# GateLoop attention and a SoLU feed-forward: second product by 32 tokens on groups of array columns, z turned without gaps, and the first chain taken per batch

## The chip, the cores and the metric

The kernel runs on one core of one Trainium2 chip, in one launch. The metric is the time of one execution on the device in microseconds (us). The engines have these names in the profile: PE is TensorE (PEld its weight loads), DVE is VectorE, ACT is ScalarE, POOL is GpSimd, SP is SyncE, which issues most of the DMA transfers. L1068 means line 1068 of the kernel before.

## What is computed

A gated linear attention with a complex decay for each of 8 heads of width 48, then a feed-forward block on its output, all in float32:

```python
B, H, S, D = 4, 8, 768, 48
mag = sqrt(a_re**2 + a_im**2)
scale = minimum(mag, 0.999) / (mag + 1e-6)
a_re_n, a_im_n = a_re * scale, a_im * scale
for t in range(S):                                   # state S_re, S_im: (B, H, D, D)
    new_re = ar * S_re - ai * S_im                   # ar, ai: step t of a_re_n, a_im_n
    new_im = ar * S_im + ai * S_re
    S_re, S_im = new_re + outer(k[t], v[t]), new_im
    y[t] = q[t] @ S_re

x = y.transpose(0, 2, 1, 3).reshape(3072, 384)
h = x @ w_in                                         # 384 -> 1024
sm = softmax(h, axis=-1)
solu = h * sm
ln = (solu - mean(solu)) / sqrt(var(solu) + 1e-6) * g_ln
out = ln @ w_out                                     # 1024 -> 384
```

## The kernel before

The work is cut into 24 chunks of 128 tokens (6 stretches of time for each of 4 batches). A group g of two chunks shares the preparation of the decays: a chain of elementwise steps between DVE and ACT that turns `a_re` and `a_im` into logarithms and angles, then running sums over the 128 tokens as products with a triangular matrix, then exponentials, cosine and sine.

```python
        def clamp():
            for nm in ("lr", "x0", "u"):
                st[nm] = tmp.tile([P, GW], FP, tag=nm, name=f"f_{nm}")      # GW = 768: two chunks of 384
            ar, ai = st["ar"], st["ai"] = flat(T["ar", g]), flat(T["ai", g])
            nc.vector.tensor_scalar(out=ar, in0=ar, scalar1=LEAST, scalar2=None, op0=OP.max, op1=OP.max,
                                    accum_out=seen[:, 1, g:g + 1])
            nc.vector.tensor_scalar(out=ai, in0=ai, scalar1=1e15, scalar2=-1e15, op0=OP.min, op1=OP.max)

        def inverse():
            nc.scalar.activation(out=st["lr"], in_=st["ar"], func=AF.Ln)
            nc.scalar.activation(out=st["x0"], in_=st["lr"], func=AF.Exp, scale=-1.0)

        def ratio():
            ar, ai, x0 = (st[nm] for nm in ("ar", "ai", "x0"))
            nc.vector.tensor_tensor(out=ai, in0=ai, in1=x0, op=OP.mult)
            nc.vector.tensor_tensor(out=x0, in0=ar, in1=x0, op=OP.mult)

        def tangent():
            ai, x0 = st["ai"], st["x0"]
            nc.vector.scalar_tensor_tensor(out=x0, in0=x0, scalar=2.0, in1=ai, op0=OP.subtract, op1=OP.mult)
            nc.vector.tensor_scalar(out=x0, in0=x0, scalar1=1.5, scalar2=-1.5, op0=OP.min, op1=OP.max)
        # [cut: square, secant, size, eps, lnm, fourth: further steps of the chain on the same 768 columns]

        def total(i):                                   # running sum of chunk i of the group
            ps = st["L", i] = ps_t.tile([P, DM], FP, tag="t", padded_shape=[P, 512], name="f_L")
            nc.tensor.matmul(out=ps, lhsT=tri, rhs=st["lr"][:, i * DM:(i + 1) * DM], start=True, stop=True)
```

For the products with k and q, both are transposed: DVE transposes blocks of 32x32 (`f_kb`), and four DMA transfers put the blocks in place (`f_kqT`). Only chunks 0 and 1 are transposed on PE. `score` and `values` then compute the attention on four groups of 32 array columns each: the outputs of four consecutive matmuls lie in four different groups of 32 partitions.

```python
        def values():
            # [cut: lists the matmuls of each of the four column groups in queues]
                    queues[p % 4].append(dict(out=y[r:r + w, c0:c0 + P], lhsT=lhsT, rhs=rhs, start=(k == 0),
                                              stop=(k == len(todo) - 1)))     # r = p % 4 * 32
            for todo in zip(*queues):
                for product in todo:
                    nc.tensor.matmul(**product)
```

The feed-forward block of a chunk n: the first product (`up`, weights x, streamed `w_in`), exp on ACT, z = h * exp on DVE (`solu`). z is transposed for the second product, in most chunks by DVE and DMA (`blocks`, `away`), in the chunks of `SHORT` on PE (`turn_z`). The second product (`down`) has the transposed z as weights and streams `w_out`. The mean of z over its 1024 columns is taken out beforehand by centring `w_out` (`mean`, `centre`), and the row scale is applied at the end (`scale`).

```python
    SHORT = [0, 1, 2, 23]

        def blocks():
            st["zb"] = zbp.tile([P, 4, 32, KF], FP, tag="zb", name="f_zb")        # KF = 8
            nc.vector.transpose(out=st["zb"].rearrange("p s t c -> p s c t"),
                                in_=st["z"].rearrange("p (c f s) -> p s c f", s=4, f=32))

        def away():
            st["zT"] = zp.tile([P, 4, 32, KF], FP, tag="zT", name="f_zT")
            for r in range(4):
                nc.sync.dma_start(out=st["zT"][:, r].rearrange("p t c -> p (t c)"),
                                  in_=st["zb"][r * 32:(r + 1) * 32].rearrange("p s t c -> p s (t c)"))

        def down(half):
            if half == 0:
                st["o"] = ps_o.tile([P, DM], FP, tag="o", padded_shape=[P, 512], name="f_o")
            for c in range(half * KF // 2, (half + 1) * KF // 2):
                nc.tensor.matmul(out=st["o"], lhsT=st["zT"][:, c] if n in SHORT else st["zT"].rearrange("p r t c -> p (r t) c")[:, :, c], rhs=w_out[:, c],
                                 start=(c == 0), stop=(c == KF - 1))
```

`mean` has eight matmuls with all 128 array columns, whose weights are one column of `g_ln` repeated:

```python
        def mean(c):
            if c == 0:
                gs = T["gs"] = const.tile([P, KF], FP, name="f_gs")
                nc.vector.tensor_scalar(out=gs, in0=g_ln, scalar1=1.0 / FF, scalar2=None, op0=OP.mult)
                T["mean"] = ps_o.tile([P, DM], FP, tag="o", padded_shape=[P, 512], name="f_mean")
            nc.tensor.matmul(out=T["mean"], lhsT=T["gs"][:, c:c + 1].to_broadcast([P, P]), rhs=w_out[:, c],
                             start=(c == 0), stop=(c == KF - 1))
```

The order in which these steps are put into the engines' queues is written down: `START`, then `EVEN` and `ODD` in turn for n = 2 to 19, then `END`. A name such as `down0:-1` stands for step `down0` of chunk n - 1, and `clamp:g2` for step `clamp` of the group two after that of n. Each engine takes its own instructions in that order. `again` and `inspect` read the weights a second time for a check of their range, and a verdict at the end selects a general version of the kernel where inputs are outside of the fast one's range.

Of the kernel before, what the change touches and what calls it, by code (L numbers as in the profile page):

```python
# [11 lines left out]
FP = mybir.dt.float32  # L12
# [503 lines left out]
load_ar:0 load_ai:0 fetch:9 fetch:13 fetch:5 clamp:0 fetch:11 inverse:0 ratio:0 raised:9 raised:13 tangent:0  # L516
fetch:2 convert:9 square:0 secant:0 size:0 fetch:0 load_k:0 raised:11 eps:0 convert:13 lnm:0 fetch:1 fourth:0
total0:0 load_ar:1 raised:0 total1:0 raised:5 decay0:0 grow1:0 grow0:0 decay1:0 convert:11 trig:0 angle:0
convert:5 convert:0 ks1:0 phase0:0 raised:2 phase1:0 last:0 ks0:0 load_q:0 nearest0:0 gain:0 nearest1:0 ends:0
load_ai:1 load_v:0 convert:2 raised:1 part0:0 part1:0 fetch:7 cos:0 convert:1 qs0:0 turn_ends:0 tot:0 clamp:1  # L520
sin:0 k2:0 exp:0 q2:0 kt0:0 inverse:1 kT0:0 qt0:0 fetch:3 k2:1 fetch:4 qs1:0 ratio:1 kt1:0 load_vr:0 qT0:0
raised:7 kT1:0 qt1:0 qT1:0 q2:1 carry:1 kt0:1 score1:0 raised:3 fetch:10 convert:7 fetch:6 kT0:1 fetch:12 add:1
fetch:8 raised:4 score0:0 load_k:1 mask0:0 load_ai:2 kt1:1 tangent:1 load_q:1 qt0:1 values:0 convert:3 qT0:1
kT1:1 qt1:1 turned_x:0 carry:0 square:1 qT1:1 secant:1 up0:0 raised:6 convert:4 up1:0 raised:8 size:1 load_ar:2
eps:1 score1:1 load_vr:2 fourth:1 raised:10 score0:1 convert:6 raised:12 convert:8 lnm:1 total0:1 convert:10
grow0:1 decay0:1 total1:1 load_v:1 grow1:1 mean:0 convert:12 ks0:1 mean:1 mean:2 mean:3 decay1:1 mean:4 exp0:0
mask0:1 mean:5 trig:1 qs0:1 angle:1 phase0:1 add:0 nearest0:1 phase1:1 solu0:0 nearest1:1 ks1:1 last:1 mean:6
centred:0 qs1:1 mean:7 values:1 clamp:2 part0:1 part1:1 zt1:0 cos:1 sin:1 centre:0 exp:1 centre:1 load_k:2
turned_x:1 zt0:0 centre:4 load_vr:1 centre:3 up0:1 inverse:2 up1:1 centre:2 centre:5 centre:7 zT0:0 k2:2
centre:6 q2:2 ratio:2 spread:0 tangent:2 load_ai:3 zT1:0 kqb:2 square:2 secant:2 kqt0:2 down0:0 size:2 k2:3 q2:3  # L530
down1:0 eps:2 exp0:1 load_q:2 lnm:2 fourth:2 total1:2 total0:2 kqb:3 solu0:1 grow1:2 decay1:2 kqt0:3 ends:1
score0:2 centred:1 grow0:2 score1:2 decay0:2 turn_ends:1 tot:1 last:2 zt0:1 mask0:2 zt1:1 load_ar:3 values:2
qs1:2 score0:3 score1:3 trig:2 angle:2 zT0:1 turned_x:2 on:2 ks1:2 zT1:1 mask0:3 phase0:2 norm:0 load_v:2
spread:1 phase1:2 ks0:2 scale:0 qs0:2 nearest0:2
"""
EVEN = """
nearest1:g1 mask0:1 carry:0 part0:g1 ks1:g1 load_q:g2 part1:g1 cos:g1 clamp:g2 up0:0 sin:g1 up1:0 load_k:g2
add:0 exp:g1 values:1 inverse:g2 k2:2 exp0:0 down0:-1 q2:2 kqb:2 turned_x:1 ratio:g2 solu0:0 tangent:g2
load_v:g2 square:g2 load_ar:g3 blocks:0 carry:1 secant:g2 size:g2 k2:3
"""  # L540
ODD = """
kqt0:1 down1:-2 q2:2 eps:g2 load_ai:g3 up0:0 up1:0 add:0 fourth:g2 centred:-1 zt0:-1 zt1:-1 zT0:-1 away:-1
norm:-2 scale:-2 again:-4 score0:1 zT1:-1 lnm:g2 store:-3 score1:1 exp0:0 spread:-1 kqb:2 solu0:0 total1:g2
decay1:g2 total0:g2 decay0:g2 mask0:1 down0:-1 blocks:0 again:-3 ends:g1 grow0:g2 qs0:g2 load_vr:g2 down1:-1
last:g2 kqt0:2 grow1:g2 centred:0 turn_ends:g1 values:1 trig:g2 inspect:-3 ks0:g2 angle:g2 score0:2 store:-2
on:g2 spread:0 inspect:-6 tot:g1 score1:2 away:0 norm:-1 phase0:g2 qs1:g2 turned_x:1 scale:-1 phase1:g2
nearest0:g2
"""
END = """
mask0:21 down0:19 nearest1:11 store:18 part0:11 part1:11 cos:11 sin:11 norm:19 k2:22 up0:20 q2:22 up1:20 exp:11  # L550
kqb:22 ks1:11 values:21 exp0:20 down1:19 solu0:20 turned_x:21 kqt0:22 score0:22 k2:23 q2:23 kqb:23 up0:21
scale:19 blocks:20 kqt0:23 score1:22 up1:21 mask0:22 exp0:21 score0:23 centred:20 away:20 solu0:21 score1:23
values:22 mask0:23 blocks:21 centred:21 spread:20 down0:20 turned_x:22 norm:20 up0:22 store:19 down1:20
spread:21 scale:20 up1:22 exp0:22 values:23 away:21 down0:21 solu0:22 turned_x:23 ends:11 blocks:22 down1:21
up0:23 norm:21 up1:23 away:22 scale:21 store:20 down0:22 centred:22 exp0:23 solu0:23 zt0:23 spread:22 centred:23
zT0:23 store:21 down1:22 zt1:23 norm:22 scale:22 down0:23 zT1:23 spread:23 down1:23 norm:23 store:22 scale:23
store:23
# [11 lines left out]
def whole(ctx, tc, flag, q, k, v, a_re, a_im, moe_w_in, moe_w_out, moe_g_ln, out):  # L569
# [55 lines left out]
    seen = const.tile([P, 3, NG], FP, name="f_seen")  # L625
# [39 lines left out]
    def weight_steps():  # L665
# [40 lines left out]
        def mean(c):  # L706
            if c == 0:
                gs = T["gs"] = const.tile([P, KF], FP, name="f_gs")
                nc.vector.tensor_scalar(out=gs, in0=g_ln, scalar1=1.0 / FF, scalar2=None, op0=OP.mult)
                T["mean"] = ps_o.tile([P, DM], FP, tag="o", padded_shape=[P, 512], name="f_mean")  # L710
            nc.tensor.matmul(out=T["mean"], lhsT=T["gs"][:, c:c + 1].to_broadcast([P, P]), rhs=w_out[:, c],
                             start=(c == 0), stop=(c == KF - 1))
# [10 lines left out]
        for c in range(KF):  # L723
            steps["mean", c], steps["centre", c] = partial(mean, c), partial(centre, c)


    def prep_steps(g):
# [3 lines left out]
        def clamp():  # L731
            for nm in ("lr", "x0", "u"):
                st[nm] = tmp.tile([P, GW], FP, tag=nm, name=f"f_{nm}")
            ar, ai = st["ar"], st["ai"] = flat(T["ar", g]), flat(T["ai", g])
            nc.vector.tensor_scalar(out=ar, in0=ar, scalar1=LEAST, scalar2=None, op0=OP.max, op1=OP.max,
                                    accum_out=seen[:, 1, g:g + 1])
            nc.vector.tensor_scalar(out=ai, in0=ai, scalar1=1e15, scalar2=-1e15, op0=OP.min, op1=OP.max)

        def inverse():
            nc.scalar.activation(out=st["lr"], in_=st["ar"], func=AF.Ln)  # L740
            nc.scalar.activation(out=st["x0"], in_=st["lr"], func=AF.Exp, scale=-1.0)


        def ratio():
            ar, ai, x0 = (st[nm] for nm in ("ar", "ai", "x0"))
            nc.vector.tensor_tensor(out=ai, in0=ai, in1=x0, op=OP.mult)
            nc.vector.tensor_tensor(out=x0, in0=ar, in1=x0, op=OP.mult)

        def tangent():
            ai, x0 = st["ai"], st["x0"]  # L750
            nc.vector.scalar_tensor_tensor(out=x0, in0=x0, scalar=2.0, in1=ai, op0=OP.subtract, op1=OP.mult)
            nc.vector.tensor_scalar(out=x0, in0=x0, scalar1=1.5, scalar2=-1.5, op0=OP.min, op1=OP.max)  # L752

        def square():
            nc.scalar.activation(out=st["ar"], in_=st["x0"], func=AF.Square)  # L755

        def secant():
            nc.scalar.activation(out=st["u"], in_=st["ar"], func=AF.Ln, bias=unit)

        def fourth():  # L760
            nc.scalar.activation(out=st["ai"], in_=st["ar"], func=AF.Square, accum_out=seen[:, 0, g:g + 1])


        def size():
            nc.vector.scalar_tensor_tensor(out=st["lr"], in0=st["u"], scalar=0.5, in1=st["lr"], op0=OP.mult, op1=OP.add)

        def eps():
            nc.scalar.activation(out=st["u"], in_=st["lr"], func=AF.Exp, scale=-1.0, bias=small)
            nc.scalar.activation(out=st["u"], in_=st["u"], func=AF.Ln, bias=unit)

        def lnm():
            nc.vector.scalar_tensor_tensor(out=st["lr"], in0=st["lr"], scalar=math.log(0.999), in1=st["u"],  # L772
                                           op0=OP.min, op1=OP.subtract)
# [42 lines left out]
        def angle():  # L816
            nc.scalar.activation(out=st["x0"], in_=st["x0"], func=AF.Arctan)
# [25 lines left out]
        def cos():  # L843
            cs = T["cs", g][:, :, 0]
            nc.scalar.activation(out=cs, in_=cs, func=AF.Sin, scale=TURN, bias=quarter)

        def sin():
            nc.scalar.activation(out=T["cs", g][:, :, 1], in_=heads(st["f"]), func=AF.Sin, scale=TURN)
            if ti < NC - 1:
                T["on", g] = two.tile([1, GW], FP, tag="on", name="f_on")  # L850
                nc.sync.dma_start(out=T["on", g], in_=st["f"][P - 1:P])

        own = dict(clamp=clamp, inverse=inverse, ratio=ratio, tangent=tangent, square=square, secant=secant,
                   fourth=fourth, size=size, eps=eps, lnm=lnm, last=last, ends=ends, trig=to_trig,
# [356 lines left out]
```

## Time and profile before

| | |
|---|---|
| time, median of 3 runs | 459.75 us (458.79 to 460.77) |
| span of the profiled execution | 457.7 us |
| busy PE / DVE / ACT / POOL | 407.6 / 366.7 / 282.9 / 50.7 us |
| second product (`f_o`, L1068): records, mean | 384, 499 ns |
| first product (`f_h`, L1009): records, mean | 288, 608 ns |
| transpose of z on DVE (L1037): count, mean | 20, 2134 ns |
| transpose of k and q on DVE (L890): count, mean | 22, 2358 ns |
| first matmul, last matmul begin at | 17.65 us, 449.77 us |

A float32 matmul leaves two records on PE, one for each pass, and each has a weight load. The ends of matmuls in the profile are modelled, so their mean durations are longer than the distance from one to the next; that distance is the better measure of what a matmul costs. A row of a group gives line, engine, operation, tiles (written <- read), shape and count, then busy time in us, mean in ns, and the idle time of the engine just ahead of these instructions with what ended it.

### The profile page before, as it was taken

The numbers are of one execution on the slowest core, as the hardware profiler recorded it, in microseconds if no ns is written. First come the engines' busy times: TensorE is split into PE (matmuls) and PEld (weight loads), VectorE is DVE, ScalarE is ACT, GpSimd is POOL, SyncE is SP. The second block draws the span as 40 slices with busy tenths as digits, with TensorE's granted clock in tenths as the row PEclk, the third lists the DMA queues.
The fourth block names the chain that finished last, engine by engine and source line by source line (L and its number), as shares of the span: only waits on it lengthen the run. The fifth ranks groups of instructions, "written<-read, shape, count | busy, mean of one in ns | idle before, by whom it ended". The sixth has DMA issues, their size and how long they took to land.

```text
span 457.7 us, 11496 instructions
## 1 busy us (share of the span) xinstructions
PE 407.6 (89%) x4764; PEld 277.0 (61%) x4764; DVE 366.7 (80%) x507; ACT 282.9 (62%) x441; POOL 50.7 (11%) x141
## 2 busy tenths in 40 slices
PE   0239979799999999999999899999999999999993
PEld 0126434555666776676677577577568668557761
DVE  5889997796799699799799699799897997573310
ACT  4989975667667567558558558656747756522140
POOL 3000000101112011021021021021021022002010
PEclk9999988899999999999999999999999999999998
DMA  8799544695788788797797787778796665153200
GB/s 242 211 206 259 113 88 103 138 193 133 169 158 223 170 171 211 170 205 186 172 187 186 162 184 200 172 170 210 164 187 167 129 147 149 36 143 79 67 31 26
DMA packets 167708, 72.27 MB, mean 158 GB/s; under 512 B 142176, under 2 KB 155488, under 8 KB 167648
## 3 DMA queue, kind: packets, MB, share of 16 engines
q1 hardware_dynamic: 167504, 71.14, 67.3%
q8 instruction: 39, 0.64, 0.6%
q10 hardware_dynamic: 144, 0.33, 0.2%
q14 instruction: 21, 0.17, 0.1%
HBM read 38.87 MB, written 4.72 MB: 95 GB/s over the span
## 4 chain that ended last, share of the span: by engine, by line
issue 46%; PE 20%; DVE 11%; POOL 7%; DMA 6%; ACT 6%; SPq 3%; DVEq 0%; POOLq 0%; ACTq 0%
PE f_o L1068 7%; PE f_h L1009 7%; DMA f_kqT<-f_kb 5%; SPq L895 3%; DVE f_kb L890 2%; PE f_y L969 2%; POOL f_less L1051 2%; POOL f_rs L1062 2%; PE f_phase L831 2%; POOL f_s L1059 1%; DVE f_kq L881 1%; PE f_score L937 1%; DMA f_ar<-in_a_re_dram 1%; POOL f_s L1060 1%; DVE f_w_out L715 1%
## 5 line engine op out<-in xcount | busy, mean ns | idle before, releaser
L1068 PE MATMUL f_o<-f_w_out,f_zT 128*128 128x384 f32 x384 | 134.8, 499 | 1.1 <-ACT f_f L834 0.7
L1009 PE MATMUL f_h<-f_w_in,f_xT 128*128 128x512 f32 x288 | 132.1, 608 | 3.3 <-ACT f_xT L1003 3.3
L1068 PEld LDWEIGHTS f_o<-f_w_out,f_zT 128*128 128x128 f32 x384 | 110.7, 294 | 16.9 <-issue 1.7
L1009 PEld LDWEIGHTS f_h<-f_w_in,f_xT 128*128 128x128 f32 x288 | 54.8, 194 | 64.5 <-issue 58.2
L890 DVE STREAM_TRANSPOSE f_kb<-f_kq 128x1536 f32<-128x1536 f32 x22 | 51.9, 2358 | 3.0 <-DMA f_kqT<-f_kb 2.7
L1051 POOL TENSOR_SCALAR f_less<-f_sum 128x1 f32<-128x1 f32 x24 | 12.0, 498 | 360.4 <-DVE f_z L1018 310.9
L941 DVE TENSOR_TENSOR f_att<-f_score,f_mats 128x1024 f32<-128x1024 f32 x24 | 29.3, 1221 | 27.0 <-PE f_score L937 27.0
L1018 DVE SCALAR_TENSOR_TENSOR f_z<-f_h,f_z 128x1024 f32<-128x1024 f32 x24 | 28.9, 1205 | 25.7 <-ACT f_z L1014 25.7
L1037 DVE STREAM_TRANSPOSE f_zb<-f_z 128x1024 f32<-128x1024 f32 x20 | 42.7, 2134 | 0.0
L937 PEld LDWEIGHTS f_score<-f_kqT 96*32 96x32 f32 x1536 | 28.9, 110 | 20.2 <-issue 15.0
L1014 ACT ACTIVATE f_z<-f_h 128x1024 f32<-128x1024 f32 x24 | 24.5, 1019 | 26.9 <-PE f_h L1009 26.9
L937 PE MATMUL f_score<-f_kqT 96*32 96x32 f32 (+3 forms) x1536 | 32.2, 235 | 8.1 <-DMA f_kqT<-f_kb 7.7
L969 PE MATMUL f_y<-f_att,f_v 128*32 128x128 f32 (+1 forms) x384 | 36.8, 275 | 0.7 <-DMA f_kqT<-f_kb 0.4
L969 PE MATMUL f_y<-f_att,f_vr 128*32 128x128 f32 x384 | 36.5, 275 | 0.0
L777 PE MATMUL f_L<-f_lr,f_mats 128*128 128x384 f32 x48 | 20.0, 541 | 18.4 <-DVE f_lr L772 18.4
L755 ACT ACTIVATE f_ar<-f_x 128x768 f32<-128x768 f32 x12 | 10.1, 844 | 38.1 <-DVE f_x L752 22.4
L969 PE MATMUL f_y<-f_kqT,f_state 96*32 96x128 f32 (+1 forms) x640 | 32.3, 272 | 0.0
L1003 ACT COPY f_xT<-f_y 128x384 f32<-128x384 f32 x24 | 11.5, 478 | 31.3 <-PE f_y L969 31.3
L1054 ACT ACTIVATE f_z<-f_z,f_less 128x1024 f32<-128x1024 f32 x24 | 27.4, 1140 | 1.2 <-DVE f_zb L1037 1.2
L834 ACT ACTIVATE f_f<-f_phase,f_bias 128x384 f32<-128x384 f32 x24 | 13.9, 581 | 21.5 <-PE f_phase L831 20.8
L969 PEld LDWEIGHTS f_y<-f_att,f_v 128*32 128x32 f32 (+1 forms) x384 | 20.0, 102 | 10.7 <-DVE f_kq L881 6.1
L1073 ACT ACTIVATE f_ot<-f_o,f_rs 128x384 f32<-128x384 f32 x24 | 13.8, 576 | 19.0 <-PE f_o L1068 9.7
(99 smaller groups left out, 627.5 us busy)
## 6 DMA issues: line engine op xcount, KB each, us to landing
f_kqT<-f_kb SPq DMA_DIRECT2D x88, 192.0 KB, 3.4
f_zT<-f_zb SPq DMA_DIRECT2D x80, 128.0 KB, 2.9
f_raw<-in_moe_w_out_dram SPq DMA_DIRECT2D x16, 384.0 KB, 5.0
f_raw<-in_moe_w_in_dram SPq DMA_DIRECT2D x12, 512.0 KB, 5.9
f_ar<-in_a_re_dram SPq DMA_DIRECT2D x12, 384.0 KB, 5.4
f_ai<-in_a_im_dram SPq DMA_DIRECT2D x12, 384.0 KB, 4.6
f_k<-in_k_dram SPq DMA_DIRECT2D x12, 384.0 KB, 4.1
f_q<-in_q_dram SPq DMA_DIRECT2D x12, 384.0 KB, 5.0
```

What stands on the lines that cost most here:

```text
L777: nc.tensor.matmul(out=ps, lhsT=tri, rhs=st["lr"][:, i * DM:(i + 1) * DM], start=True, stop=True)
L890: nc.vector.transpose(out=t, in_=T["kq", c].rearrange("p n h (f j) -> p j (n h) f", j=3))
L937: nc.tensor.matmul(out=scores[r0:r0 + 32, x, r:], lhsT=QK[:, r // 32, x], rhs=QK[:, r // 32:, H + x], start=True, stop=True)
L941: nc.vector.tensor_tensor(out=st["att"].rearrange("p (i u) t -> p i u t", u=2), in0=scores.rearrange("p (i u) t -> p i u t", u=2), in1=mat ...
L969: nc.tensor.matmul(**product)
L1009: nc.tensor.matmul(out=st["h"][:, half * 512:(half + 1) * 512], lhsT=st["xT"][:, c * P:(c + 1) * P], rhs=w_in[:, c, half * 512:(half + 1) ...
L1014: nc.scalar.activation(out=st["z"], in_=st["h"], func=AF.Exp, accum_out=sums[:, n:n + 1])
L1018: nc.vector.scalar_tensor_tensor(out=st["z"], in0=st["h"], scalar=1.0, in1=st["z"], op0=OP.mult, op1=OP.mult, accum_out=st["sum"][:, 0:1])
L1037: nc.vector.transpose(out=st["zb"].rearrange("p s t c -> p s c t"), in_=st["z"].rearrange("p (c f s) -> p s c f", s=4, f=32))
L1051: nc.gpsimd.tensor_scalar(out=st["less"], in0=st["sum"][:, 0:1], scalar1=-1.0 / FF, scalar2=None, op0=OP.mult)
L1054: nc.scalar.activation(out=st["z"], in_=st["z"], func=AF.Square, bias=st["less"], accum_out=st["sum"][:, 1:2])
L1068: nc.tensor.matmul(out=st["o"], lhsT=st["zT"][:, c] if n in SHORT else st["zT"].rearrange("p r t c -> p (r t) c")[:, :, c], rhs=w_out[:, c ...
```

## The change

It has four parts. The first moves the second product to groups of 32 tokens: for each of the 8 pieces c of the inner dimension, four matmuls with 32 columns of weights replace one with 128, each in its own group of array columns and output partitions. This lets the transposed z lie as `[4, KF, 32]`, so that the DVE transpose writes without gaps and each weight load reads 32 neighbouring elements. The second part takes the chain of group 0 in two halves, one for each batch (`clampa`, `clampb` and so on), so that one half can begin on an engine while the other half is on another. The third computes the mean in four groups of array columns, two matmuls in each, and adds the four parts with one further matmul against ones. The fourth is a new order of all steps. A counter for the range check gets one more column, and the transfer `onward`, which was part of `sin`, is a step of its own.

```diff
-            st["zb"] = zbp.tile([P, 4, 32, KF], FP, tag="zb", name="f_zb")
-            nc.vector.transpose(out=st["zb"].rearrange("p s t c -> p s c t"),
-                                in_=st["z"].rearrange("p (c f s) -> p s c f", s=4, f=32))
+            st["zb"] = zbp.tile([P, 4, KF, 32], FP, tag="zb", name="f_zb")
+            nc.vector.transpose(out=st["zb"], in_=st["z"].rearrange("p (c f s) -> p s c f", s=4, f=32))
 # [cut: away has the same four transfers, with (c t) in place of (t c)]
             for c in range(half * KF // 2, (half + 1) * KF // 2):
-                nc.tensor.matmul(out=st["o"], lhsT=st["zT"][:, c] if n in SHORT else st["zT"].rearrange("p r t c -> p (r t) c")[:, :, c], rhs=w_out[:, c],
-                                 start=(c == 0), stop=(c == KF - 1))
+                if n in SHORT:
+                    parts = [(slice(0, P), st["zT"][:, c])]
+                else:
+                    parts = [(slice(r * 32, r * 32 + 32), st["zT"][:, r, c]) for r in range(4)]
+                for rows, zT in parts:
+                    nc.tensor.matmul(out=st["o"][rows], lhsT=zT, rhs=w_out[:, c], start=(c == 0), stop=(c == KF - 1))
 # [cut]
-                nc.vector.tensor_scalar(out=gs, in0=g_ln, scalar1=1.0 / FF, scalar2=None, op0=OP.mult)
-                T["mean"] = ps_o.tile([P, DM], FP, tag="o", padded_shape=[P, 512], name="f_mean")
-            nc.tensor.matmul(out=T["mean"], lhsT=T["gs"][:, c:c + 1].to_broadcast([P, P]), rhs=w_out[:, c],
-                             start=(c == 0), stop=(c == KF - 1))
+                nc.vector.tensor_scalar(out=gs, in0=g_ln, scalar1=1.0 / (32 * FF), scalar2=None, op0=OP.mult)
+                T["parts"] = ps_t.tile([P, DM], FP, tag="t", padded_shape=[P, 512], name="f_parts")
+            r = c % 4 * 32
+            nc.tensor.matmul(out=T["parts"][r:r + 32], lhsT=T["gs"][:, c:c + 1].to_broadcast([P, 32]), rhs=w_out[:, c],
+                             start=(c < 4), stop=(c >= 4))
+
+        def sum_mean():
+            parts = ffp.tile([P, DM], FP, tag="ot", name="f_meanp")
+            nc.scalar.copy(out=parts, in_=T["parts"])
+            T["mean"] = ps_o.tile([P, DM], FP, tag="o", padded_shape=[P, 512], name="f_mean")
+            nc.tensor.matmul(out=T["mean"], lhsT=ones, rhs=parts, start=True, stop=True)
 # [cut]
-        def inverse():
-            nc.scalar.activation(out=st["lr"], in_=st["ar"], func=AF.Ln)
-            nc.scalar.activation(out=st["x0"], in_=st["lr"], func=AF.Exp, scale=-1.0)
+        def inverse(cs):
+            nc.scalar.activation(out=st["lr"][:, cs], in_=st["ar"][:, cs], func=AF.Ln)
+            nc.scalar.activation(out=st["x0"][:, cs], in_=st["lr"][:, cs], func=AF.Exp, scale=-1.0)
 # [cut: the other steps of the chain take cs in the same way]
+        for i in range(GB) if g == 0 else [None]:
+            cs, hs = (slice(0, GW), slice(0, GH)) if i is None else (slice(i * DM, (i + 1) * DM), slice(i * H, (i + 1) * H))
+            for nm, f in chain.items():
+                more = {"o": NG} if i == 1 and nm in ("clamp", "fourth") else {}
+                own[nm + ("" if i is None else "ab"[i])] = partial(f, cs, **more)
 # [cut: the order]
```

In the loop, the steps on PE for one pair of chunks (n even, `|` between steps) stand in this order before:

```
up:n | values:n+1 | down0:n-1 | carry:n+1 | down1:n-1 | up:n+1 | score:n+2 | L of g2 | down:n | tot | values:n+2 | score:n+3 | phase | carry:n+2
```

and in this order after:

```
up1:n | values:n+1 | down:n-1 | carry:n+1 | up:n+1 | score:n+2 | L of g2 | down:n | tot | values:n+2 | score:n+3 | phase | carry:n+2 | up0:n+2
```

## The prediction

> **What bounds the kernel now.** I read the page's busy times first, then the same engines in stretches of time, then TensorE's (PE's) timeline over one period of the loop, then the groups of instructions, and the waits last. The first view is the page's part 2, busy tenths in 40 slices of 11.4 us:
>
> ```profile
> PE   0239979799999999999999899999999999999993
> ...
> DVE  5889997796799699799799699799897997573310
> ...
> PEclk9999988899999999999999999999999999999998
> ```
>
> PE is nearly full from the fourth slice to the last but one, with dips in the sixth and eighth; before that VectorE (DVE) is the busier of the two, and in slices six to eight the granted clock falls below 9 tenths. So there are three stages: a start of some 84 us, a loop to about 388 us, and a tail. The next view gives busy us by stretch (columns: length, then busy time of PE, PE's weight loads, DVE, ScalarE, GpSimd, the clock, the DMA share, GB/s):
>
> ```profile
> 5.50:17.60 12.10, 0.00 (x0) 0.00 (x0) 9.65 (x16) 9.77 (x15) 0.00 (x0) 1.00 1.04 317
> ...
> 65.30:73.50 8.20, 8.18 (x12) 3.48 (x13) 8.10 (x9) 5.43 (x8) 0.00 (x0) 0.64 0.33 64
> ...
> 184.70:218.20 33.50, 33.03 (x420) 23.55 (x419) 30.81 (x41) 21.81 (x35) 4.09 (x11) 1.00 0.82 187
> ```
>
> In the loop PE is busy 33.03 of 33.50 us, DVE 30.81, ScalarE 21.81. A pair of chunks takes 32.98 us (score to score, 188.24 to 221.22 in the timeline), and PE has about 0.4 us of it free. At the start PE has no matmul until 17.6 us, and twelve matmul records of the first product take 8.2 us at clock 0.64. The timeline of PE over a period (start, length, line, count; two passes per fp32 matmul, so two records each):
>
> ```profile
> 199.04 2.97 PE L1068 MATMUL f_o<-f_w_out,f_zT 128*128 128x384 f32 x8
> 201.95 0.88 PE L977 MATMUL f_d<-f_v,f_kq 128*32 128x48 f32 x48
> 202.76 2.98 PE L1068 MATMUL f_o<-f_w_out,f_zT 128*128 128x384 f32 x8
> 205.57 5.31 PE L1009 MATMUL f_h<-f_w_in,f_xT 128*128 128x512 f32 x12
> ...
> 213.47 5.32 PE L1068 MATMUL f_o<-f_w_out,f_zT 128*128 128x384 f32 x16
> 218.72 0.22 PE L810 MATMUL f_tot<-f_mats,f_e 16*96 16x16 f32 x1
> ```
>
> The ends are modelled, so I take start to next start. The second product of one chunk as a single run of 16 records takes 218.72 - 213.47 = 5.25 us, 328 ns a record; cut into two runs of 8 it takes 2.91 + 2.81 = 5.72 us. Both follow a product in column groups, so each of the two cut runs pays some 0.2 to 0.3 us to begin. Within a run nothing is lost: the rate is set by the 384 streamed columns. The groups (busy us, mean ns) show why the beginning is dear:
>
> ```profile
> L1068 PEld LDWEIGHTS f_o<-f_w_out,f_zT 128*128 128x128 f32 x384 | 110.7, 294 | 16.9 <-issue 1.7 <-ACT f_z L1014 1.6 <-ACT f_f L834 1.3
> L1009 PEld LDWEIGHTS f_h<-f_w_in,f_xT 128*128 128x128 f32 x288 | 54.8, 194 | 64.5 <-issue 58.2 <-ACT f_xT L1003 3.6
> L890 DVE STREAM_TRANSPOSE f_kb<-f_kq 128x1536 f32<-128x1536 f32 x22 | 51.9, 2358 | 3.0 <-DMA f_kqT<-f_kb 2.7
> L1037 DVE STREAM_TRANSPOSE f_zb<-f_z 128x1024 f32<-128x1024 f32 x20 | 42.7, 2134 | 0.0
> ```
>
> A weight load of z (every eighth element of a row) takes 294 ns against 194 for packed weights of the same size; hidden under a 323 ns stream, but bare at the start of a run. The transpose of z costs 2134/1024 = 2.08 ns an element, that of k and q, which writes without gaps, 2358/1536 = 1.54.
>
> **What the Trainium skill says.** "SBUF — State Buffer", section "Door 1: The DMA port swizzle", gives lines of 16 bytes in SBUF and a penalty for each access that goes to a new line. That agrees with both pairs of numbers above; it also warns that z is still read at a step of 16 bytes, so only the write side improves. "TensorEngine Tiling (Array Packing)", "Key Properties", says that tiles work independently and that a change of mode drains the array. The trace agrees: the output y in four groups (128*32, 128 columns) has 64 records in 1.89 us (197.15 to 199.04), 118 ns per step of four where one 128-column stream at the down product's rate would take 109, so the four do run together; and a first product of 12 records takes 5.35 us after a grouped product and 5.24 after an ungrouped one, 0.1 us per change of mode. "TensorE: Matmul & The Clock Gate", Part 1, says that after idling TensorE is at half clock until it has been busy again for some us; the stretch at clock 0.64 follows a 3.3 us gap in PE's timeline.
>
> **The change, part by part.**
>
> *Second product, loop.* 16 records of 128 columns become 64 of 32 columns, in 16 steps of four. If a step costs what the longer stream costs plus y's excess (about 328 + 9 = 337 ns) a chunk takes 5.39 us; if only the stream counts, 5.25. In the new order both halves stand together, the cut runs are gone, and before them stands a grouped product in one case of two. Two chunks: 5.72 + 5.25 = 10.97 before, 10.5 to 10.8 after: 0.2 to 0.5 us a pair, not a fourfold gain, since the array was full before. Everything of this lies on PE, which is the path.
>
> *z without gaps.* With the rate of k and q, 1024 x 1.54 = 1.58 us; I take 1.6. That frees 0.53 us of DVE per chunk, 20 x 0.53 = 10.6 us in all, 1.06 in a pair. DVE is not the path in the loop, so this buys slack (30.4 of 32.98 us becomes 29.3), with which the transposes can be ready earlier. The copy by DMA keeps its size, 1 KB pieces on both sides.
>
> *New order, loop.* What it can win is the free PE time, 0.38 to 0.47 us a pair, ahead of a score that waits for turned k and q. I give it two thirds, 0.3. With 0.4 for the product the pair comes to 32.3 us, and nine pairs give 9 x 0.7 = 6.3 us.
>
> *First chain per batch.* From the first DVE instruction (5.50) to the first matmul (17.65) the first chain is 12.15 us: six DVE operations of 0.96, one of 0.56, and six on ScalarE of 0.84 to 0.94, on each other's results. A 384-wide operation takes about 0.55 on DVE and 0.49 on ScalarE (the rows of the 384-wide products and exponentials), so one half needs 6 x 0.55 + 0.35 + 6 x 0.49 = 6.6 us, and the other fits into the gaps. The first running sum should start near 12.5 to 13.5 us, 4 to 5 earlier. But from there DVE is nearly the limit: between 5.5 and 84 us it is busy 70.2 of 78.5, so at most 8.3 us can be had, less about 1.1 for seven doubled fixed costs of 0.16. I count 3.5.
>
> *Mean in four groups.* Before, 16 records of 128 columns of weights at 323 ns, 5.65 us. After, 16 records in four groups, 4 steps of about 0.33, then one full matmul, 0.65: 2.0 us, and a ScalarE copy of about 0.48. That is 3.6 us of PE off the start, but there DVE is often ahead of it; together with the chance that the 2.9 us lost to the low clock goes, I count 1.5.
>
> *Tail.* From 385 us PE has some 2.6 us of gaps, and three chunks use the new product. I count 1.5. The last 8 us, from the last product at 449.8 to the end of the store, stay.
>
> Sum: 6.3 + 3.5 + 1.5 + 1.5 = 12.8, and 459.75 - 12.8 is about 447.
>
> **Rivals.** (a) Issue bound: 64 small records with a weight load each might not come fast enough. Against it: score records come at 1.26 us / 64 = 20 ns each, and here a step leaves 80 ns for each. If it held, a chunk would take 6 us or more and the loop would gain nothing: about 455. (b) The loop stays where it is because another wait takes over: scores wait for turned k and q by DMA (median 3.4 us to landing, four issues of about 0.6 us ahead of it), and a faster PE asks for them earlier. DVE, at 29.3 of 32.3 us, has little room either. Then only start and tail gain: 452. (c) The start gains more than I allow. PE has about 33 us without work before 84 us, the new order may put work there, and VectorE may hand work on to the loop, where it has new slack; then 440. (d) The column groups bring new changes of mode, at 0.1 us each some 1 us in nine pairs: a small debit, within the range.
>
> **Range and chances.** Start and tail together I put at 3 to 11 us, the loop at 2 to 10; both at their ends at once is unlikely. That gives 439.5 to 454.5 with 447 in the middle. Faster by over 2% means below 450.55, 3.5 us above my middle with a spread of about 6: a chance of 0.73. Within 2% 0.25, slower by over 2% 0.02, which would need rival (a) and a bad order together.
>
> **What will show it.** The second product: 64 records in about 5.3 us from its start to the next line's, and no short run of it. The transpose of z: about 1600 ns. Pair period: about 32.3 us from score to score. First running sum: 12.5 to 13.5 us. Mean: about 2 us in all. DVE's total about 356 us. The prediction is wrong if a step of four takes much more than 337 ns, if the z transpose stays above 2 us (reads at 16 bytes being the cost), or if the first loop period starts no earlier than before although the first chain is shorter.

## The result and the profile after

The changed kernel takes 448.03 us (median of 4 runs, 447.14 to 448.91), against 459.48 us of the kernel before beside it: a ratio of 0.975 with a 95% interval of 0.972 to 0.978. Beside a later group of experiments it measured 0.972 (0.968 to 0.975). The span of its profile is 445.3 us, 12.4 us less than before.

Part 2 of the page of the changed kernel, busy tenths in slices of 11.1 us:

```profile
PE   0238966989999999999999999999999999999993
...
DVE  5689999778999999899999899899999999764310
...
PEclk9985898899999999999999999999999999999997
```

PE is full from the tenth slice on without a dip. The start is not better: PE has low slices until the seventh, and the clock is low in slices three to five and again in seven and eight.

To say where the time went I cut both profiles at the same three points of the work: the fourth and the twelfth pair's angle product (`f_phase`) and the last matmul, `f_count`. All times are starts in PE's timeline, in us.

| | start: to the 4th `f_phase` | loop: 4th to 12th, 8 pairs | tail: 12th to `f_count` |
|---|---|---|---|
| before | 122.98 | 265.27 | 61.52 |
| after | 123.02 | 255.58 | 58.76 |
| difference | 0.0 | -9.7 | -2.8 |

The rest, from `f_count` to the end, is 7.9 us in both. So the loop and the tail gave everything and the start gave nothing. A start is not the same in every profile of one kernel: in a second profile of the changed kernel the fourth `f_phase` comes at 121.75 us and the loop takes 256.8 us. Busy us by stretch for the loop, first of the kernel before, then of the changed one (columns as in the prediction):

```profile
123.00:388.20 265.20, 260.62 (x3338) 184.92 (x3335) 240.25 (x308) 171.08 (x264) 34.11 (x91) 1.00 0.78 177
```

```profile
123.00:378.60 255.60, 255.60 (x4111) 137.97 (x4104) 242.99 (x309) 169.00 (x265) 45.76 (x88) 1.00 0.81 184
```

PE was idle for 4.6 us in eight pairs and is now idle for none; its own work fell by 5.0 us, 0.63 a pair. DVE has no less to do than before. One period of PE's timeline in the changed kernel, the lines that answer to those of the prediction:

```profile
196.35 5.34 PE L1093 MATMUL f_o<-f_w_out,f_zT 128*32 128x384 f32 x64
201.51 0.86 PE L998 MATMUL f_d<-f_v,f_kq 128*32 128x48 f32 x48
202.29 5.42 PE L1030 MATMUL f_h<-f_w_in,f_xT 128*128 128x512 f32 x12
...
208.78 2.78 PE L1093 MATMUL f_o<-f_w_out,f_zT 128*32 128x384 f32 x32
211.49 1.56 PE L789 MATMUL f_L<-f_lr,f_mats 128*128 128x384 f32 x4
212.98 2.79 PE L1093 MATMUL f_o<-f_w_out,f_zT 128*32 128x384 f32 x32
215.69 0.22 PE L822 MATMUL f_tot<-f_mats,f_e 16*96 16x16 f32 x1
```

Start to next start, 64 records take 201.51 - 196.35 = 5.16 us, 322 ns per step of four; the other chunk's two halves, which stand on both sides of the running sum, take 2.71 + 2.71. A pair's second product is 10.58 us in place of 10.97. The groups (busy us, mean ns):

```profile
L1058 DVE STREAM_TRANSPOSE f_zb<-f_z 128x1024 f32<-128x1024 f32 x20 | 43.5, 2175 | 0.1
L1093 PEld LDWEIGHTS f_o<-f_w_out,f_zT 128*32 128x32 f32 x1280 | 40.4, 110 | 56.0 <-issue 56.0
```

Weight loads of 110 ns overlap one another (40.4 us busy for 320 steps of four, 126 ns a step) and leave the stream of 322 ns a step undisturbed. But the transpose of z, which now writes without gaps, takes 2175 ns; it took 2134.

### The profile page after: what moved, and what is told of

It reads as the page before. It is cut to its first block, busy times and chain, and to the rows that moved or that the text cites. A ratio compares the mean times of both kernels' runs of the same rounds, so it can differ in the third digit from the quotient of the medians.

```text
span 445.3 us, 13426 instructions
## 1 busy us (share of the span) xinstructions
PE 400.0 (90%) x5726; PEld 219.5 (49%) x5726; DVE 371.4 (83%) x516; ACT 282.6 (63%) x453; POOL 67.2 (15%) x141
## 4 chain that ended last, share of the span: by engine, by line
PE 82%; DMA 5%; ACT 4%; DVE 4%; SPq 2%; issue 1%; POOL 0%; DVEq 0%; ACTq 0%
PE f_o L1093 29%; PE f_h L1030 26%; PE f_y L990 9%; PE f_score L958 6%; PE f_L L789 4%; PE f_phase L843 4%; PE f_d L998 3%; DMA f_kqT<-f_kb 2%; DMA f_raw<-in_moe_w_in_dram 2%; DVE f_kq L902 1%; DMA f_raw<-in_moe_w_out_dram 1%; SPq L916 1%; ACT f_bits L690 1%; ACT f_bits L688 1%; SPq L650 1%
## 5 line engine op out<-in xcount | busy, mean ns | idle before, releaser
L1093 PE MATMUL f_o<-f_w_out,f_zT 128*32 128x384 f32 (+1 forms) x1344 | 133.2, 489 | 0.2 <-ACT f_zT L1052 0.2
L1030 PE MATMUL f_h<-f_w_in,f_xT 128*128 128x512 f32 x288 | 130.4, 600 | 0.0
L1093 PEld LDWEIGHTS f_o<-f_w_out,f_zT 128*32 128x32 f32 (+1 forms) x1344 | 53.3, 114 | 65.2 <-issue 58.0
L1030 PEld LDWEIGHTS f_h<-f_w_in,f_xT 128*128 128x128 f32 x288 | 52.6, 190 | 59.4 <-issue 57.2
L1058 DVE STREAM_TRANSPOSE f_zb<-f_z 128x1024 f32<-128x1024 f32 x20 | 43.5, 2175 | 0.1
L958 PEld LDWEIGHTS f_score<-f_kqT 96*32 96x32 f32 x1536 | 31.8, 114 | 16.0 <-issue 8.9
L958 PE MATMUL f_score<-f_kqT 96*32 96x96 f32 (+3 forms) x1536 | 34.5, 243 | 5.1 <-DMA f_kqT<-f_kb 5.1
L990 PE MATMUL f_y<-f_att,f_v 128*16 128x128 f32 (+1 forms) x384 | 37.4, 281 | 0.6 <-DVE f_att L962 0.6
L1080 POOL TENSOR_SCALAR f_s<-f_s,f_sum 128x1 f32<-128x1 f32 x24 | 15.1, 627 | 75.8 <-ACT f_z L1074 75.1
L793 ACT ACTIVATE f_ai<-f_L 128x384 f32<-128x384 f32 x24 | 12.0, 499 | 22.8 <-PE f_L L789 22.8
L990 PEld LDWEIGHTS f_y<-f_att,f_v 128*16 128x16 f32 (+1 forms) x384 | 20.9, 104 | 10.0 <-issue 8.7
```

Of the source, the lines that this page charges most:

```text
L958: nc.tensor.matmul(out=scores[r0:r0 + 32, x, r:], lhsT=QK[:, r // 32, x], rhs=QK[:, r // 32:, H + x], start=True, stop=True)
L1030: nc.tensor.matmul(out=st["h"][:, half * 512:(half + 1) * 512], lhsT=st["xT"][:, c * P:(c + 1) * P], rhs=w_in[:, c, half * 512:(half + 1) ...
L1058: nc.vector.transpose(out=st["zb"], in_=st["z"].rearrange("p (c f s) -> p s c f", s=4, f=32))
L1093: nc.tensor.matmul(out=st["o"][rows], lhsT=zT, rhs=w_out[:, c], start=(c == 0), stop=(c == KF - 1))
```

## The experiments

The times are medians; ratios are to the kernel before, run on the same chip, with 95% intervals. "After" without a qualifier is the changed kernel.

**1. Grouping undone, new order kept (e1).** In the changed kernel:

```diff
-            nc.vector.transpose(out=st["zb"], in_=st["z"].rearrange("p (c f s) -> p s c f", s=4, f=32))
+            nc.vector.transpose(out=st["zb"].rearrange("p s t c -> p s c t"),
+                                in_=st["z"].rearrange("p (c f s) -> p s c f", s=4, f=32))
 # [cut: the tiles of zb and zT and the four transfers, as in the kernel before]
-                for rows, zT in parts:
-                    nc.tensor.matmul(out=st["o"][rows], lhsT=zT, rhs=w_out[:, c], start=(c == 0), stop=(c == KF - 1))
+                nc.tensor.matmul(out=st["o"], lhsT=st["zT"][:, c] if n in SHORT else st["zT"].rearrange("p r t c -> p (r t) c")[:, :, c], rhs=w_out[:, c],
+                                 start=(c == 0), stop=(c == KF - 1))
```

> The changed kernel with its new order, but with the second product in 128 columns and z laid out as before. If grouping saves PE time by itself, about 0.4 us a pair in the product and 0.2 us in the outputs y that follow a change of mode, ten pairs give some 4 to 6 us: 452 to 454 us. If the new order alone made the loop faster, the time stays at 448 to 449. If grouping is all of it, 457 to 460. The transpose of z should stay at 2.1 to 2.2 us either way, as it did in the change.

449.05 us, ratio 0.977 (0.973 to 0.980). This is close to the second case. The busy times of its loop, same columns:

```profile
121.00:380.00 259.00, 259.00 (x3340) 185.32 (x3335) 242.41 (x308) 168.95 (x265) 43.17 (x88) 1.00 0.80 181
```

The new order alone leaves PE no idle time in the loop (265.3 to 259.0 us). The second product takes 10.97 us a pair here, as before the change. Grouping takes another 3.4 us of PE work, 0.43 a pair. In the time of the whole the difference to the changed kernel, 1 to 2 us, is within the intervals; this profile's start, in the same order, was 2 us shorter. The transpose of z takes 2106 ns here.

**2. Grouping alone, old order (e2).** The kernel before with the new `blocks`, `away` and `down`, nothing else.

> The kernel before with its old order and old start, and only the second product in groups of 32 with the new layout of z. If the two halves of the product, each after another grouped product, lose the 0.2 to 0.3 us with which they began, a pair is 0.5 us shorter and the time 454 to 456 us. If the wait for turned k and q takes over instead, it stays at 458 to 460.

458.5 us, ratio 0.997 (0.995 to 1.000): some 1 us. Its loop is 259.3 us, 6.0 less than before, but its start is 2.0 us and its tail 2.1 us longer. The time is that of the second case, but the loop does what the first says:

```profile
125.00:384.20 259.20, 256.72 (x4105) 138.41 (x4104) 242.18 (x308) 172.02 (x264) 34.53 (x91) 1.00 0.80 181
```

PE's work falls by 3.9 us and its idle time from 4.6 to 2.5. Two lines of the tail in PE's timeline, last column what the idle time waited for:

```profile
386.93 2.77 PE L1072 MATMUL f_o<-f_w_out,f_zT 128*32 128x384 f32 x26 [0.40 <-DMA f_zT<-f_zb]
...
408.62 1.33 PE L937 MATMUL f_score<-f_kqT 96*32 96x128 f32 x64 [1.25 <-DMA f_kqT<-f_kb]
```

In the tail PE's waits for turned z, k and q grow from 1.0 to 2.5 us, so there the faster product does ask for them before they have landed; in the loop they fall from 4.2 to 2.2 us. The gain in the loop is real, and the tail gives back a third of it. What makes the start longer was not found; starts of one order differ by as much between profiles (120.96 us in e7, 123.02 in the changed kernel).

**3. First chain whole (e3).**

```diff
-        for i in range(GB) if g == 0 else [None]:
+        for i in [None]:
```

with `clamp:0` in the place of `clampb:0` and so on in the order.

> The changed kernel with the first chain taken over both batches at once, in the place of the first half. If the halves brought nothing, because conversions of weights stand between the links of the chain in the engines' queues, the time stays within 1 us of 448. If the halves hid a loss that the new order would otherwise have, it is 451 to 453.

449.62 us, ratio 0.976 (0.973 to 0.979). By the ratios that is 0.7 us slower than after, or 2.1 us than its second measurement, with intervals that overlap; it is nearer to the first case: halving the chain is worth nothing that these runs can tell. The first running sum begins at 18.61 us here, at 18.15 in the changed kernel and at 17.65 before.

**4. Mean ungrouped (e4).** `mean` as before, eight matmuls of 128 columns, in the new order.

> The changed kernel with the mean in eight matmuls of 128 columns, 3.5 us more on PE near 62 us. If the time saved there is lost again in the 4 us wait for turned k and q at 71 us, the total stays at 447 to 449, and the half clock after that wait may even go. If PE is the path there, it is 451 to 452.

451.92 us, ratio 0.983 (0.980 to 0.986): by the ratios 3.8 us slower than after (5.2 than its second measurement), the second case. PE's lines of the mean, first in the changed kernel, then in e4:

```profile
61.56 1.51 PE L714 MATMUL f_parts<-f_w_out,f_gs 128*32 128x384 f32 x16 [1.32 <-DVE f_gs L711]
...
64.64 0.91 PE L721 MATMUL f_mean<-f_meanp,f_mats 128*128 128x384 f32 x2
```

```profile
61.67 5.43 PE L712 MATMUL f_mean<-f_w_out,f_gs 128*128 128x384 f32 x16 [2.13 <-DVE f_gs L710]
```

To the next start that is 1.32 + 0.75 us in place of 5.36, and this saving is on the path of the new order. Between 48 and 72 us DVE is busy 20.14 us in this run and 23.10 in the changed kernel; in e4 it waits 0.9 us for the mean before it centres `w_out`, and PE then 2.1 us for the centred `w_out`.

**5. Chain first (e8).** Conversions of pieces 5, 13 and 9 of the weights moved behind the first chain, in the order alone.

> The changed kernel with three of the early weight conversions (raised and convert of pieces 5, 13 and 9) put behind the first chain in the queues of ScalarE and VectorE. If these conversions stand in the way of the halved chain, the first running sum begins at 13.5 to 15 us in place of 18.15. Whether that reaches the end: if VectorE's total work and the half clock limit the start, the total stays at 446.5 to 449; if the first chain is the path, it falls to 443 to 445.

450.69 us, ratio 0.978 (0.974 to 0.982): no gain, and above both cases. ScalarE in the chain, first in the changed kernel, then in e8:

```profile
10.64 0.76 ACT L688 ACTIVATE f_bits<-f_raw,f_bias 128x512 f32<-128x512 uint32 x1 [1.47 <-DMA f_raw<-in_moe_w_in_dram]
11.44 0.72 ACT L690 ACTIVATE f_bits<-f_bits,f_bias 128x512 int32<-128x512 f32 x1
12.06 0.51 ACT L767 ACTIVATE f_ar<-f_x 128x384 f32<-128x384 f32 x1
```

```profile
10.43 0.52 ACT L767 ACTIVATE f_ar<-f_x 128x384 f32<-128x384 f32 x1 [1.24 <-DVE f_x L764]
```

`f_x` is ready at 10.38 us in the changed kernel, but ScalarE first waits for a piece of weights and converts it. PE's timeline in e8:

```profile
15.45 2.93 PE L789 MATMUL f_L<-f_lr,f_mats 128*128 128x384 f32 x4 [15.45 <-DVE f_lr L784]
21.23 2.93 PE L843 MATMUL f_phase<-f_x,f_mats 128*128 128x384 f32 x4 [2.85 <-ACT f_x L829]
34.74 3.45 PE L923 MATMUL f_turned<-f_mats,f_kq 128*96 128x128 f32 x16 [10.59 <-DVE f_kq L902]
```

The conversions did stand in the chain: without them the first sum begins 2.7 us earlier, though not in 13.5 to 15 us. But the next work of PE, the turns of k and q, begins at 34.74 us, against 32.58 in the changed kernel, after a wait of 10.6 us for DVE. The conversions have only moved, and DVE comes no earlier to what PE needs.

**6. Matmuls of no use in PE's long waits (e5, e6).** Five matmuls of the identity with constants, added work whose result nothing reads: in e5 ahead of the scores of chunk 2, in e6 after the first angle product.

```diff
 # [cut: takes a tile ps of PSUM]
+            for _ in range(k):
+                nc.tensor.matmul(out=ps, lhsT=ident, rhs=mats[:, 0:3].rearrange("p n t -> p (n t)"), start=True, stop=True)
```

> The changed kernel with five matmuls of no use (identity against constants, 384 columns, about 3.2 us) in PE's 4 us wait ahead of the scores of chunk 2 at 71 us. If the half clock that follows this wait (a first run of the second product in 4.9 in place of 2.6 us, scores in 2.3 in place of 1.3) is a loss on the path, it goes and the total falls by 2.5 to 3.5 us, to 444.5 to 446. If something else holds PE there, the total stays at 448.

> The changed kernel with the same five matmuls in PE's wait of 5.7 us at 27 us, before the first turns of k and q. The half clock from 30 to 47 us should go, about 4 us of PE. If VectorE is the path between 41 and 75 us (busy 17.9 of 19.0 us), little of that reaches the end: 446 to 448.5. If PE is the path from the first turns on, 444 to 445.

e5: 446.86 us, ratio 0.971 (0.967 to 0.976), between its two cases; e6: 449.59 us, 0.976 (0.972 to 0.980), above both of its cases. Neither can be told from after by its time. The place of e6 tells little: between 24 and 48 us the clock is 0.79 in e6 and 0.64 in the changed kernel, but 1.00 in the second profile of the changed kernel, which has no added work. PE's timeline at the place of e5, first in the changed kernel, then in e5:

```profile
75.10 2.36 PE L958 MATMUL f_score<-f_kqT 96*32 96x128 f32 x64 [3.96 <-DMA f_kqT<-f_kb]
77.40 4.95 PE L1093 MATMUL f_o<-f_w_out,f_zT 128*128 128x384 f32 x8
```

```profile
70.27 3.39 PE L739 MATMUL f_warm<-f_mats 128*128 128x384 f32 x10
74.25 1.33 PE L966 MATMUL f_score<-f_kqT 96*32 96x128 f32 x64 [0.58 <-DMA f_kqT<-f_kb]
75.51 2.85 PE L1101 MATMUL f_o<-f_w_out,f_zT 128*128 128x384 f32 x8
```

The mechanism holds at the place of e5: with PE kept busy, scores take 1.3 in place of 2.3 us and half a product 2.8 in place of 4.9. The fourth `f_phase` begins at 119.34 us, 3.7 earlier (2.4 against the second profile). But the loop takes 257.8 in place of 255.6 us, since scores in its first pairs now wait, with no releaser that the profile shows, and 1.4 us of the span remain.

**7. z read straight (e7).** The transpose reads neighbouring columns; which column meets which row of `w_out` within a piece of 128 is left out of account, the amount of work is the same.

```diff
-            nc.vector.transpose(out=st["zb"], in_=st["z"].rearrange("p (c f s) -> p s c f", s=4, f=32))
+            nc.vector.transpose(out=st["zb"], in_=st["z"].rearrange("p (c s f) -> p s c f", s=4, f=32))
```

> The changed kernel with the transpose of z reading neighbouring elements in place of every fourth (the columns of z then meet other rows of w_out within a piece of 128, so this leaves the right matching of columns out; the work is the same). If the step of the reads sets the time of the transpose, it falls from 2175 ns to 1100 to 1600. If not, it stays at 2100 to 2200. Either way PE is the path in the loop and the total stays at 446 to 448.5; 440 or less would mean that VectorE was the path.

446.62 us, ratio 0.970 (0.966 to 0.974); the group of the transpose:

```profile
L1058 DVE STREAM_TRANSPOSE f_zb<-f_z 128x1024 f32<-128x1024 f32 x20 | 24.8, 1239 | 0.1
```

The step of the reads costs 936 ns of 2175. Beside such reads the gaps in the writes cost nothing (2134 ns with them, 2175 without); gaps in the writes beside neighbouring reads were not tried. DVE's 18.7 us less bring at most 1 or 2 us of time, since PE fills the loop (255.9 us).

**8. The same with all of the work, and with e5 (e9, e10).** The rows of `w_out` and `g_ln` are loaded in the matching order. The four chunks that PE turns have to match too; there the first product streams `w_in` with steps of 32 columns.

```diff
 # [cut: the loads, and the transpose as in e7]
+                if n in SHORT:
+                    o, w = o.rearrange("p (k f s) -> p k f s", s=4, f=32), w.rearrange("p (k s f) -> p k f s", s=4, f=32)
```

Beside them ran the changed kernel once more.

> The changed kernel as it is, beside the two that follow: 447 to 450 us, a pair of chunks in 31.95 us.

> The changed kernel with the transpose of z reading neighbouring elements, and with the rows of w_out and of g_ln loaded in the order that matches (in the four chunks turned on PE the first product picks the columns of w_in in that order), so that all of the work is done. Transpose of z 1240 ns, DVE total 18 to 19 us less. If PE alone is the path in the loop, the time is that of the changed kernel within 1.5 us; if VectorE's load also costs, 444 to 446.

> The same with the five matmuls of no use ahead of the scores of chunk 2. In the run with these matmuls alone the loop began 3.7 us earlier but lost 2.2 us in its first four pairs, where scores waited. If that was VectorE's backlog, the cheaper transpose takes it away and the whole 3 to 4 us remain: 443 to 445 us, with no free PE time in the loop. If it was the loads or transfers, 446 to 447 with the same waits in the loop.

After again: 447.5 us, 0.972 (0.968 to 0.975), a pair in 32.10 us. e9: 461.81 us, 1.004 (1.002 to 1.006); e10: 464.94 us, 1.011 (1.007 to 1.014). Both expectations of these two missed, for a reason that stands in PE's timeline of e9:

```profile
45.95 10.64 PE L1037 MATMUL f_h<-f_w_in,f_xT 128*128 128x512 f32 x12
```

The first product of a chunk takes 10.5 us where it reads `w_in` at steps of 32 columns (128 bytes), four columns and then the next four, against 5.2 to 5.4 in order. Four chunks pay that: start and tail are 6.3 and 5.3 us longer than after, the loop (256.5 us) is not. e10 has a result all the same: its loop has the waits of e5 (257.8 us, 1.5 us of waits without a releaser against 1.6), with the transpose at 1236 ns. So it was not DVE's transpose that held the scores back.

**9. Old order of the start (e12).** The changed kernel with the old `START`, the chain whole, the mean's matmuls in one place, the additional steps at the end; loop and tail in the new order.

> The changed kernel with the old order of the start (the first chain whole, the mean in four groups done at one place, the steps that the new start does in addition put at its end), and the new order of the loop and the tail. If the new order of the start is what cost the gain there, the loop's fourth group begins some 3 us earlier than at 122 to 123 us and the total is 444 to 446. If the start is bound by VectorE and by waits that both orders have, it stays at 447 to 450.

453.27 us, ratio 0.984 (0.981 to 0.988), outside both cases. The fourth `f_phase` begins at 126.83 us. PE waits 1.5 us at the mean, which now stands in one place, and 7.8 in place of 5.3 us for the angle products, so this does not rank the two orders as they stand; it only shows that the old start does not fit better.

## Why the prediction was right, and where it was not

The predicted time was 447 us, the measured 448.03. The sum was right and its four terms were not; too little for the loop and the tail and too much for the start cancelled, and that is luck. Start and tail together were put at 3 to 11 us and brought 2.8; the loop was put at 2 to 10 us and brought 9.7 in eight pairs. One of the signs of being wrong that the prediction names came in full: the transpose of z stays above 2 us. Another came in half: the loop begins no earlier, but the first chain is no shorter either.

**Second product, loop: right.** 0.4 us a pair was taken, 10.97 to 10.58 is 0.39. The step of four costs 322 ns, not 337: no excess at all. Rival (a), the rate of issue, is out: the weight loads of 110 ns hide. What the cut runs lost at their beginning has two parts. The kernel before has one such run, between the same neighbours, in a chunk that PE turned, where the weights are packed:

```profile
98.56 2.85 PE L1068 MATMUL f_o<-f_w_out,f_zT 128*128 128x384 f32 x8
101.34 0.88 PE L977 MATMUL f_d<-f_v,f_kq 128*32 128x48 f32 x48
```

It takes 2.78 us, where the run at 199.04 in the prediction, with weights at steps of 32 bytes, takes 2.91; eight records at 323 ns would be 2.58. So the gaps in the weights account for 0.13 of the 0.33 us, the change to and from column groups for the rest. No run packs the weights without grouping in the loop. One thing was read wrongly: the product of the even chunk is not in one piece in the new order but stands on both sides of the running sums (`down0:n | L of g2 | down1:n`), 5.42 us in place of 5.16.

**New order, loop: under-sized.** It was given two thirds of the free PE time of a pair, 0.3. It took all: 4.6 us in eight pairs, 0.57 each, more than the 0.38 to 0.47 that I had read from two pairs. The two parts are not separate sums: grouping alone takes 6.0 us off the loop (e2), the order alone 6.2 (e1), both 9.7, since either shortens PE's waits. The remaining 0.24 a pair of PE work is outputs and scores that come out shorter beside another grouped product (1.79 in place of 1.90 us, one score 1.14 in place of 1.26), less what running sums and a first product pay. I had booked changes of mode as a small debit (rival d); the balance is a gain. A pair went from 33.16 to 31.95 us, 1.21 in place of 0.7.

**z without gaps: failed.** The step "with the rate of k and q, 1.6 us" took the write side to be the difference between the two transposes. It is the read side: z is read at steps of 16 bytes, as e7 shows with 1239 ns, and k and q at steps of 12 (`j=3` in L890). An element costs 2.12 ns at 16 bytes, 1.54 at 12 and 1.21 without a step. The Trainium skill ("SBUF — State Buffer", section "Door 1: The DMA port swizzle"), which I had quoted for both sides, agrees with the trace for the reads; for these writes (2134 ns at steps of 32 bytes, 2175 without) the trace shows no penalty. It did not spoil the total because DVE is not the path in the loop.

**First chain per batch: failed.** 12.5 to 13.5 us was predicted for the first running sum, 18.15 came. The working counted the chain's own links; in the queues of ScalarE and DVE weight conversions stand between them, and e8 shows they account for 2.7 us. Even without them the first half takes 10.0 us (5.44 to 15.45) and not 6.6: DVE waits 1.25 us for `a_im` to land, and steps of the other half stand between its own. It would not have helped: e3 and e8 leave the time where it was. From 24 to 72 us DVE is busy 45.2 of 48 us before and 44.9 after, and the change takes no work from it there. I had named that limit and still counted 3.5 us.

**Mean in four groups: size right, credit wrong.** 2.0 us predicted, 1.32 + 0.75 measured. In the new order all of it is on the path (e4), so it should have counted for 3.6. As the start in sum is unchanged, the rest of the new start must have cost about as much. What that is stays open. PE waits more: from 24 us to the fourth `f_phase` it is idle for 16.3 us in the changed kernel and 19.6 in its second profile, against 14.6 before. The half clock is not shown to be a part: between 24 and 96 us 12.0 us of PE's clock (the length of a stretch times the share of the clock that was not granted) were withheld in the changed kernel, 3.4 in its second profile and 5.0 before, and the fourth `f_phase` came at 123.02, 121.75 and 122.98; but e1, with the same order of the start and 12.0 us withheld, has it at 121.01.

**Tail: under-sized.** 1.5 us counted, 2.8 measured. e1, with the new order alone, has a tail of 58.95 us, so this is the order, which leaves 0.2 us of gaps where there were 2.1.

Rival (b), another wait that takes over, did not come in the changed kernel, nor in the loop of e2, where the old order meets the faster product; it comes in the tail of e2, and in e5, where the loop begins earlier. Why scores wait in e5 is not settled; DVE's transpose of z is excluded by e10.

## What to carry to other kernels

A full array gained nothing in streaming from column groups, but packed weights, and neighbours in the same mode, gained tenths of a us per product; in the old order a gain of 6.0 us in the loop left some 1 us of the whole, so look at the order of start and tail too. Before an access pattern is changed, measure reads and writes apart: here the reads cost 43% of the instruction and the gaps in the writes, beside them, nothing. This start, with several full engines, was not shortened by splitting one chain in it; ask first which engine is full there and whether the change takes work from it.

## What the runs showed of the hardware

Reading the streamed operand of a float32 product at steps of 128 bytes halved the rate: 10.5 us for twelve records of 512 columns, against 5.2 to 5.4 (e9). A transpose on DVE pays for steps of 16 bytes on its reads, 2175 against 1239 ns for 1024 elements, and beside such reads not for steps of 32 bytes on its writes, 2134 against 2175. Grouped matmuls of 384 columns run at 322 ns per step of four, the rate of one ungrouped record.
